# Attention and feed-forward kernel: another token order, merged tails and a different load list for the first batch

## The chip, the cores and the metric

The kernel runs on one core of a Trainium2 chip. The metric is device time in microseconds (us); three runs of the kernel before gave 718.85, 719.02 and 719.22 us, median 719.02 us. Inputs and outputs lie in the chip's memory (HBM). A core has a matrix engine (TensorE, PE), a vector engine (VectorE, DVE), an activation engine (ScalarE, ACT), a general engine (GpSimd, POOL) and a queue engine (SyncE, SP). Loads are issued from SP's and ACT's instruction streams and carried by the core's 16 DMA engines.

## The reference, cut to what matters

There are 8 batches, 8 heads, 576 tokens, head width 64, and 32 memory slots. All is float32.

```python
a   = exp(phi - max over tokens)            # phi: batch, head, token, slot
a   = a / (sum of a over tokens + 1e-9)
k_m = sum over tokens of a[token, slot] * k[token, :]      # v_m likewise with v
s   = q @ k_m.T / sqrt(64);  p = softmax(s over slots)
x   = p @ v_m                              # 4608 rows of 512 = 8 heads x 64
out = square(relu(x @ w_in)) @ w_out       # w_in 512x2048, w_out 2048x512
```

The sums over tokens do not care in which order the tokens come, so long as `phi`, `k` and `v` are taken in the same order.

## The kernel before, in words

Each batch has 576 tokens, cut in five chunks: four of 128 tokens (a token per partition) and a tail of 64 tokens (`rows(4)` is 64). `e_sb` holds `phi` as 128 partitions x 5 chunks x 256, where the 256 columns are two halves (`qd` 0 and 1) of four heads x 32 slots. `kv` holds for each batch and half of the heads 576 tokens x 4 heads x 128 (k beside v), so that a token of one half is 2 KB in a row.

For batch 0 the start is written out by hand in the string `order` (L957), whose letters step through generators:

- `e` is `exp_phi` (L166): the maximum over chunks on DVE (L170, L175), two transposes on PE (L180), a reduce (L185), a broadcast by matmul (L190), then per chunk an addition on DVE (L199) and an exponential on ACT (L201).
- `m` is `task_mem`, which runs `memories` (L322): sums of the chunks on DVE (L332, L335), 40 small matmuls (recorded as 80) for the sums over tokens (L350), first those of half 0 and then of half 1, chunk by chunk, the denominators (L357), and a division and transposes.
- `d0` to `d3` decode pieces of `w_in` (ACT L581 and L584, DVE L586 to L594, an addition at L601); `a0` is the attention of the first tokens (`first_softmax`: DVE L487 to L512, ACT L497 and L517); `u0` makes the first product for the feed-forward part.

Engines take their instructions in the order in which the program lists them. `spin` (L144) puts fillers on PE, matmuls whose result nobody reads: `spin(n, x, k=4)` is n matmuls over k blocks of 128 columns. Before the first transpose there are `spin(3, ident)` and `spin(1, ident, k=2)`, 14 blocks.

The first loads come from the list `loads` (L910): `load_phi` for batch 0 (SP takes the four whole chunks, ACT the 64-row tail), then `first_kv` for each half (three loads: chunks 0 and 1, chunks 2 and 3, tail; on ACT, SP, ACT for half 0, and on SP, SP, ACT for half 1), then the first piece of `w_in`, four loads of `q`, and further pieces of the weights. That is two loads of `phi` and six of `kv` ahead of the first weights. The data of `kv` go to tiles that are used for other things later (`u_hi3`, `u_lo3`, `u_hi4`, `wo4`, `wo5`, `wo6`). A tail tile has its unused 64 partitions set to zero by POOL (`fill`, L106). Each tail load goes to partitions 0 to 63.

After the start, steps of the feed-forward part (L677, L720, L728) run on PE by a fixed plan (`plan`, `early`, `late`), with the tasks of the following batches between them.

Of the kernel before, what the change touches and what calls it, by code (L numbers as in the profile page):

```python
# [8 lines left out]
F32 = mybir.dt.float32  # L9
# [3 lines left out]
AF = mybir.ActivationFunctionType  # L13
ALU = mybir.AluOpType
# [10 lines left out]
def attn_moe_kernel(ctx: ExitStack, tc: tile.TileContext, qT, kv, phi, w_in, w_out, outT):  # L25
# [20 lines left out]
    D = 64  # L46
# [12 lines left out]
    def rows(c):  # L59
        return min(P, S - c * P)  # L60
# [45 lines left out]
    def fill(c, t):  # L106
        if rows(c) < P:
            nc.gpsimd.memset(t[rows(c):], 0.0)
        if t.shape[-1] == CW:
            nc.gpsimd.memset(t[:rows(c), :, 2 * D:], 1.0)  # L110

    def fill_all():
        for c in range(NCH):
            fill(c, kvb[c])
            if rows(c) < P:
                nc.gpsimd.memset(e_sb[rows(c):, c], 0.0)

    ones = const.tile([P, CW - 2 * D], F32, name="ones")
    nc.gpsimd.memset(ones, 1.0)
# [24 lines left out]
    def spin(n, x, h=None, k=4):  # L144

        if h is None:
            h = ps_h.tile([P, 512], F32, name="h")
        for _ in range(n):
            nc.tensor.matmul(  # L149
                h[:, :k * P], x, ident[:, None, :].broadcast_to([P, k, P]), start=True, stop=True  # L150
            )

    def load_phi(b, nc_q=nc.sync):
        nfull = S // P
        assert b == 0 or ("read", b - 1) in ready
        nc.sync.dma_start(out=e_sb[:, :nfull], in_=phi[b, :nfull * P].rearrange("(c p) x -> p c x", p=P))
        if b > 1:
            for qd in range(NQ):
                nc_q.dma_start(
                    out=e_sb[D * qd:D * (qd + 1), nfull, :P], in_=phi[b, nfull * P:, qd * P:(qd + 1) * P]  # L160
                )
            return [e_sb[:, c] for c in range(nfull)] + [e_sb[:, nfull, :P]]
        nc_q.dma_start(out=e_sb[:rows(nfull), nfull], in_=phi[b, nfull * P:])
        return [e_sb[:rows(c), c] for c in range(NCH)]

    def exp_phi(b, e):  # L166

        w = NQ * P
        mx = one.tile([P, w], F32, name="phi_mx")
        nc.vector.tensor_tensor(out=mx, in0=e[0], in1=e[1], op=ALU.max)  # L170
        for x in e[2:]:
            n = x.shape[0]
            if fine and not starting:
                yield True
            nc.vector.tensor_tensor(out=mx[:n], in0=mx[:n], in1=x, op=ALU.max)  # L175
        yield
        ps = new_ps()
        tp, bc = bank(ps, 0), bank(ps, 1)
        for qd in range(NQ):
            nc.tensor.transpose(tp[:, qd * P:(qd + 1) * P], mx[:, qd * P:(qd + 1) * P], ident)  # L180
        if starting:
            spin(1, ident, k=2)
        yield
        nmx = work.tile([P, NQ], F32, name="nmx")
        nc.vector.tensor_reduce(  # L185
            out=nmx, in_=tp[:, :w].rearrange("p (q x) -> p q x", q=NQ), axis=AX.X, op=ALU.max, negate=True
        )
        yield
        for qd in range(NQ):
            nc.tensor.matmul(  # L190
                bc[:, qd * P:(qd + 1) * P], nmx[:, qd:qd + 1].broadcast_to([P, P]), ident,
                start=True, stop=True,
            )
        if starting:
            spin(2, nmx[:, :1].broadcast_to([P, P]))
        yield
        for x in e:
            n = x.shape[0]
            nc.vector.tensor_tensor(out=x, in0=x, in1=bc[:n, :w], op=ALU.add)  # L199
            if starting:  # L200
                nc.scalar.activation(x, x, AF.Exp)  # L201
        done_ps(ps)
        if starting:
            ready.add(("phi", b))
            return
        yield
        nfull = S // P
        nc.scalar.activation(e_sb[:, :nfull], e_sb[:, :nfull], AF.Exp)
        if nfull < NCH:
            nc.scalar.activation(e[nfull], e[nfull], AF.Exp)  # L210
        ready.add(("phi", b))

    def exp_phi_blocks(b, e):

        w = NQ * P
        nb = w // M
        mx = one.tile([P, w], F32, name="phi_mx")
        nc.vector.tensor_tensor(out=mx, in0=e[0], in1=e[1], op=ALU.max)
        for x in e[2:-1]:
            nc.vector.tensor_tensor(out=mx, in0=mx, in1=x, op=ALU.max)  # L220
        at = [(slice(D * qd, D * (qd + 1)), slice(P * qd, P * (qd + 1))) for qd in range(NQ)]
        for hs, cs in at:
            nc.vector.tensor_tensor(out=mx[hs, cs], in0=mx[hs, cs], in1=e[-1][hs], op=ALU.max)
        yield
        tr = one.tile([P, w], F32, name="at")
        nc.vector.transpose(tr, mx)
        top = work.tile([P, nb], F32, name="top")
        nc.vector.tensor_reduce(out=top, in_=tr.rearrange("p (k x) -> p k x", k=nb), axis=AX.X, op=ALU.max)
        yield
        for g in range(1, P // M):  # L230
            nc.vector.tensor_tensor(out=top[:M], in0=top[:M], in1=top[M * g:M * (g + 1)], op=ALU.max)
        for g in range(1, P // M):
            nc.vector.tensor_copy(top[M * g:M * (g + 1)], top[:M])
        yield
        nc.vector.tensor_copy(tr.rearrange("p (k x) -> p k x", k=nb), top[:, :, None].broadcast_to([P, nb, M]))
        nc.vector.transpose(mx, tr)
        yield
        for x in e[:-1]:
            nc.vector.tensor_tensor(out=x, in0=x, in1=mx, op=ALU.subtract)
        for hs, cs in at:  # L240
            nc.vector.tensor_tensor(out=e[-1][hs], in0=e[-1][hs], in1=mx[hs, cs], op=ALU.subtract)
        yield
        nfull = S // P
        nc.scalar.activation(e_sb[:, :nfull], e_sb[:, :nfull], AF.Exp)
        nc.scalar.activation(e[nfull], e[nfull], AF.Exp)
        ready.add(("phi", b))

    def load_kv(b, qd, lent=None):

        got = []  # L250
        for c in range(NCH):
            if lent:
                t = lent(c)
            elif qd and b > 1 and rows(c) < P:
                nc.sync.dma_start(out=kvb[c][D:, :, :2 * D], in_=kv[b, qd, c * P:])
                got.append(kvb[c])
                continue
            elif qd:

                name, bufs = ("tmp", 3) if c < 3 else ("low", 2)  # L260
                if b == 2 and c < 3:
                    if not c:
                        w1 = const.tile([P, 3, 4, CW], F32, name="w1")
                    t = w1[:, c]
                else:
                    t = work.tile([P, 4, CW], F32, name=name, bufs=bufs)
            else:
                t = kvb[c]
                assert c not in kv_used
                kv_used.add(c)  # L270
            if qd:
                fill(c, t)
            elif b == 2 and rows(c) < P:
                nc.gpsimd.memset(t[rows(c):, :, 2 * D:], 1.0)
            nc.sync.dma_start(out=t[:rows(c), :, :2 * D], in_=kv[b, qd, c * P:c * P + rows(c)])
            got.append(t)
        return got

# [43 lines left out]
    def memories(b, e, kvs, mem):  # L322
# [7 lines left out]
        if b == 0:  # L330
            total = one.tile([P, NQ * P], F32, name="phi_mx")
            nc.vector.tensor_tensor(out=total, in0=e[0], in1=e[1], op=ALU.add)  # L332
            for c in range(2, NCH):
                n = rows(c)
                nc.vector.tensor_tensor(out=total[:n], in0=total[:n], in1=e[c][:n], op=ALU.add)  # L335
        for qd, kvt in kvs.items():
            if b and kvt[0].shape[-1] < CW:
                for c, y in enumerate(kvt):
# [542 lines left out]
    st = state[0]  # L881
    kvs = {}

    def first_kv(qd):

        names = (("u_hi3", "u_lo3", "u_hi4"), ("wo4", "wo5", "wo6"))[qd]
        queues = ((nc.scalar, nc.sync, nc.scalar), (nc.sync, nc.sync, nc.scalar))[qd]
        got = []
        for name, nc_q in zip(names, queues):
            c = len(got)  # L890
            t = const.tile([P, 2, 4, 2 * D], F32, name=name)
            n = min(2, S // P - c)
            if n:
                x = kv[0, qd, c * P:(c + n) * P].rearrange("(c p) h x -> p c h x", p=P)
                nc_q.dma_start(out=t[:, :n], in_=x)
                got += [t[:, k] for k in range(n)]
            else:
                fill(c, t[:, 0])
                nc_q.dma_start(out=t[:rows(c), 0], in_=kv[0, qd, c * P:])
                got.append(t[:, 0])  # L900
        kvs[qd] = got

    def first_phi():
        st["phi"] = load_phi(0, nc.scalar)
# [2 lines left out]
    def next_kv():  # L907
# [1 line left out]

    loads = [  # L910
        (first_phi,),
        (first_kv, 0),
        (first_kv, 1),
        (fetch_w_in, 0, 0),
        (task_q, 0, 0),
        (task_q, 0, 1),
# [24 lines left out]

    nc.scalar.activation(ones[:1, :1], ones[:1, :1], AF.Exp, scale=0.0)
    spin(3, ident)
    spin(1, ident, k=2)
    start = {
        "e": lambda: exp_phi(0, st["phi"]),
        "m": lambda: task_mem(0, kvs),
# [283 lines left out]
```

## Time and profile before

| | |
|---|---|
| Runs | 718.85, 719.02, 719.22 us |
| Profiled execution, first to last instruction (span) | 717.0 us |
| Median of the runs less that span | 2.0 us |
| PE busy | 708.0 us (99%) |
| DVE / ACT / POOL busy | 388.6 / 332.6 / 197.6 us |
| Moved by DMA | 89.50 MB |

The profiled execution's own time is given only as its span; what lies around the span is the difference to the runs. PE's busy time takes in the fillers. Times within the trace are counted from the span's start.

### The profile page before, as it was taken

How to read it: one execution, taken by the hardware profiler on the slowest of the kernel's cores; microseconds unless marked ns; L12 is line 12 of the kernel's file. 1: busy time of each engine (PE TensorE's matmuls, PEld its weight loads, DVE VectorE, ACT ScalarE, POOL GpSimd, SP SyncE). 2: the span in 40 equal slices, each digit the busy share in tenths (PEclk: the TensorE clock that was granted, in tenths of full speed). 3: DMA queues.
4: the chain of work that ended last, by engine and by line, in shares of the span. 5: the costliest groups of instructions: out<-in, count | busy, mean ns of one | idle time of the engine just before them, and what ended most of it. 6: DMA issues, size and time to landing. Idle time of an engine off the chain costs nothing.

```text
span 717.0 us, 13710 instructions
## 1 busy us (share of the span) xinstructions
PE 708.0 (99%) x5380; PEld 617.4 (86%) x5380; DVE 388.6 (54%) x835; ACT 332.6 (46%) x644; POOL 197.6 (28%) x221
## 2 busy tenths in 40 slices
PE   9899999999999999999999999999999999999998
PEld 4477798987989998888999999888899899888997
DVE  4978787987686644445472645533573445221211
ACT  2648887875454443323442444323454244332332
POOL 1222103012320133222332334222433243223332
PEclk9999999999999999999999999999999999999999
DMA  9992435331876712083411911146221222100101
GB/s 305 390 351 93 147 138 139 123 122 37 253 243 217 199 59 69 28 230 120 147 59 43 306 69 37 59 145 171 94 89 67 90 96 96 59 1 1 59 1 37
DMA packets 63281, 89.50 MB, mean 125 GB/s; under 512 B 3888, under 2 KB 52272, under 8 KB 59632
## 3 DMA queue, kind: packets, MB, share of 16 engines
q1 hardware_dynamic: 62416, 87.52, 37.9%
q10 hardware_dynamic: 800, 1.10, 0.5%
q8 instruction: 42, 0.69, 0.4%
q14 instruction: 23, 0.19, 0.1%
HBM read 74.97 MB, written 13.63 MB: 124 GB/s over the span
## 4 chain that ended last, share of the span: by engine, by line
PE 93%; DMA 2%; DVE 2%; ACT 1%; issue 0%; POOL 0%; ACTq 0%; SPq 0%; DVEq 0%
PE acc L728 53%; PE h L677 28%; PE ps_m L408 5%; PE acc L720 3%; PE h L286 2%; DMA wo<-in_w_in 1%; DMA u_hi<-in_kv 1%; PE h L408 1%; PE h L149 1%; PE ps_m L350 0%; POOL a_lo L472 0%; DVE at L468 0%; DVE st L465 0%; DVE sm L454 0%; DVE u_lo L560 0%
## 5 line engine op out<-in xcount | busy, mean ns | idle before, releaser
L685 ACT ACTIVATE r_room<-h 128x320 f32<-128x320 f32 (+2 forms) x200 | 95.4, 477 | 262.9 <-PE h L677 256.9
L691 DVE TENSOR_TENSOR g_room<-h,r_room 128x320 f32<-128x320 f32 (+1 forms) x148 | 82.5, 558 | 238.7 <-ACT r_room L685 229.7
L728 PE MATMUL acc<-g_hi,wo 128*128 128x320 f32 (+1 forms) x1024 | 175.5, 308 | 0.0
L728 PEld LDWEIGHTS acc<-g_hi,wo 128*128 128x128 f32 x1024 | 155.6, 188 | 6.1 <-ACT r_room L685 2.5
L705 POOL TENSOR_TENSOR g_lo<-g_room,g_hi 128x320 fp32r<-128x320 f32 (+1 forms) x102 | 89.9, 882 | 223.9 <-DVE g_room L691 166.6
L728 PE MATMUL acc<-o,wo 128*128 128x512 f32 x576 | 139.9, 391 | 0.0
L728 PEld LDWEIGHTS acc<-o,wo 128*128 128x128 f32 x576 | 105.2, 188 | 21.5 <-issue 1.7
L677 PE MATMUL h<-a_hi,u_hi 128*128 128x320 f32 (+1 forms) x448 | 100.9, 306 | 0.7 <-ACT u_hi L558 0.7
L705 POOL TENSOR_TENSOR o<-g_room,o 128x512 fp32r<-128x512 f32 x48 | 62.0, 1291 | 143.7 <-PE acc L728 97.0
L728 PE MATMUL acc<-g_lo,wo 128*128 128x320 f32 (+1 forms) x512 | 100.7, 307 | 0.0
L677 PE MATMUL h<-a_hi,u_lo 128*128 128x320 f32 (+1 forms) x448 | 96.3, 296 | 0.8 <-DVE u_lo L560 0.8
L677 PE MATMUL h<-a_lo,u_hi 128*128 128x320 f32 (+1 forms) x448 | 96.1, 296 | 0.1
L677 PEld LDWEIGHTS h<-a_hi,u_hi 128*128 128x128 f32 x448 | 74.8, 189 | 23.6 <-DVE st L428 9.2
L728 PEld LDWEIGHTS acc<-g_lo,wo 128*128 128x128 f32 x512 | 81.5, 188 | 0.0
L677 PEld LDWEIGHTS h<-a_hi,u_lo 128*128 128x128 f32 x448 | 72.0, 189 | 1.9 <-DVE u_lo L560 1.9
L677 PEld LDWEIGHTS h<-a_lo,u_hi 128*128 128x128 f32 x448 | 72.2, 189 | 0.4 <-POOL a_lo L472 0.4
L701 ACT ACTIVATE g_hi<-r_room 128x320 fp32r<-128x320 f32 (+1 forms) x128 | 59.8, 467 | 7.6
L701 ACT ACTIVATE o<-r_room 128x512 fp32r<-128x512 f32 x48 | 30.4, 633 | 42.4 <-PE acc L728 42.0
L560 DVE TENSOR_TENSOR u_lo<-ps_m,u_hi 128x1024 fp32r<-128x1024 f32 (+1 forms) x29 | 34.3, 1183 | 4.6 <-ACT u_hi L558 4.1
L408 PE MATMUL ps_m<-w,mem 64*32 64x512 f32 (+1 forms) x528 | 35.6, 582 | 0.9 <-POOL w L601 0.9
L720 PE MATMUL acc<-g_hi,wo 128*128 128x256 f32 (+1 forms) x128 | 34.1, 409 | 0.0
L720 PEld LDWEIGHTS acc<-g_hi,wo 128*128 128x128 f32 x128 | 23.2, 190 | 7.0 <-issue 2.0
(175 smaller groups left out, 716.4 us busy)
## 6 DMA issues: line engine op xcount, KB each, us to landing
w<-w_f SPq DMA_DIRECT2D x24, 1024.0 KB, 4.8
wo<-in_w_in SPq DMA_DIRECT2D x16, 512.0 KB, 8.1
wo<-in_w_out SPq DMA_DIRECT2D x16, 512.0 KB, 8.0
kvb<-in_kv SPq DMA_DIRECT2D x28, 256.0 KB, 6.3
q_sb<-in_q SPq DMA_DIRECT2D x16, 320.0 KB, 6.2
out_t<-o SPq DMA_DIRECT2D x30, 160.0 KB, 1.9
e_sb<-in_phi SPq DMA_DIRECT2D x8, 512.0 KB, 6.9
w_f<-w SPq DMA_DIRECT2D x4, 1024.0 KB, 5.7
```

The source lines that it names most:

```text
L149: nc.tensor.matmul(h[:, :k * P], x, ident[:, None, :].broadcast_to([P, k, P]), start=True, stop=True)
L286: nc.tensor.matmul(acc[qd][M * j:M * (j + 1), :CW], e_sb[hs, c, col + M * j:col + M * (j + 1)], kvs[qd][c][hs, j, :], start=(c == 0), stop ...
L408: nc.tensor.matmul(out[half][M * pr:M * (pr + 1), :y.shape[-1]], mem[hs, x, pr], y, start=True, stop=True)
L560: nc.vector.tensor_tensor(out=u_lo[:, :, n0:n1], in0=ps[:, :, :n1 - n0], in1=u_hi[:, :, n0:n1].bitcast(F32), op=ALU.subtract)
L677: nc.tensor.matmul(h[:, at:at + n], u[:, qd, fs], x[:, qd], start=(i == 0), stop=(i == len(todo) - 1))
L685: nc.scalar.activation(r, h[:, :T], AF.Relu)
L691: nc.vector.tensor_tensor(out=g, in0=h[:, :T], in1=r, op=ALU.mult)
L701: nc.scalar.activation(g_hi, r, AF.Square)
L705: adder.tensor_tensor(out=g_lo, in0=g, in1=g_hi.bitcast(F32), op=ALU.subtract)
L720: nc.tensor.matmul(acc[e][:, :T], wo[f][:, e * P:(e + 1) * P], g_hi, start=first, stop=last)
L728: nc.tensor.matmul(acc[e][:, :T], wo[f][:, w, e * P:(e + 1) * P], x, start=first and x is g_hi and w == 0, stop=last and x is g_lo,)
```

## The change

For every batch the four whole chunks of a half take their tokens in another order: partition p holds tokens 4p to 4p+3 instead of p, 128+p, 256+p, 384+p. The tail of 64 tokens stays the tail.

For batch 0 besides: `phi` comes in two loads of two chunks each (SP and ACT), and its tail as one load to 128 partitions, half 0 of the columns on partitions 0 to 63, half 1 on 64 to 127, in a small tile `at`. The `kv` tails of both halves come as one load to 128 partitions (`u_hi4`). The maximum is taken two chunks at a time, and the tail is treated apart, one half of the partitions at a time. The exponentials of the tail are written into `e_sb` beside zeros that POOL sets. `spin(1, ident, k=2)` at the start is gone, which leaves 12 blocks.

```diff
 def fill_all():  ...
-                nc.gpsimd.memset(e_sb[rows(c):, c], 0.0)
+                nc.gpsimd.memset(e_sb[D:, c, :P], 0.0)
+                nc.gpsimd.memset(e_sb[:D, c, P:], 0.0)
 def load_phi(b, nc_q=nc.sync):  ...
-        nc.sync.dma_start(out=e_sb[:, :nfull], in_=phi[b, :nfull * P].rearrange("(c p) x -> p c x", p=P))
+        x = phi[b, :nfull * P].rearrange("(p c) x -> p c x", p=P)
+        if b == 0:
+            for i, q in enumerate((nc.sync, nc_q)):
+                q.dma_start(out=e_sb[:, 2 * i:2 * i + 2], in_=x[:, 2 * i:2 * i + 2])
+            tail = one.tile([P, P], F32, name="at")
+            nc.sync.dma_start(out=tail, in_=phi[b, nfull * P:].rearrange("t (q x) -> q t x", q=NQ))
+            return [e_sb[:, c] for c in range(nfull)] + [tail]
+        nc.sync.dma_start(out=e_sb[:, :nfull], in_=x)
+        if b == 1:
+            nc.gpsimd.memset(e_sb[D:, nfull, P:], 0.0)
 def exp_phi(b, e):  ...
+        if b == 0:
+            two = one.tile([P, 2, w], F32, name="st")
+            nc.vector.tensor_tensor(out=two, in0=e_sb[:, 0:2], in1=e_sb[:, 2:4], op=ALU.max)
+            nc.vector.tensor_tensor(out=mx, in0=two[:, 0], in1=two[:, 1], op=ALU.max)
+            for hs, cs in halves:
+                nc.vector.tensor_tensor(out=mx[hs, cs], in0=mx[hs, cs], in1=e[-1][hs], op=ALU.max)
 ...
+            if x.shape[-1] < w:
+                for hs, cs in halves:
+                    nc.vector.tensor_tensor(out=x[hs], in0=x[hs], in1=bc[hs, cs], op=ALU.add)
+                    nc.scalar.activation(e_sb[hs, NCH - 1, cs], x[hs], AF.Exp)
+                continue
+    def tokens_of(b, qd, c):
+        nfull = S // P
+        if c == nfull:
+            return kv[b, qd, c * P:]
+        return kv[b, qd, :nfull * P].rearrange("(p c) h x -> p c h x", p=P)[:, c]
 def load_kv(b, qd, lent=None):  ...
-            nc.sync.dma_start(out=t[:rows(c), :, :2 * D], in_=kv[b, qd, c * P:c * P + rows(c)])
+            nc.sync.dma_start(out=t[:rows(c), :, :2 * D], in_=tokens_of(b, qd, c))
-    def first_kv(qd):
 ...
+    def first_kv():
+        nfull = S // P
+        tail = const.tile([P, 4, 2 * D], F32, name="u_hi4")
+        nc.scalar.dma_start(out=tail, in_=kv[0, :, nfull * P:])
+        for qd, names in enumerate((("u_hi3", "u_lo3"), ("wo4", "wo5"))):
+            x = kv[0, qd, :nfull * P].rearrange("(p c) h x -> p c h x", p=P)
+            got = []
+            for i, (nc_q, name) in enumerate(zip((nc.scalar, nc.sync), names)):
+                t = const.tile([P, 2, 4, 2 * D], F32, name=name)
+                nc_q.dma_start(out=t, in_=x[:, 2 * i:2 * i + 2])
+                got += [t[:, k] for k in range(2)]
+            kvs[qd] = got + [tail]
-    spin(1, ident, k=2)
```

## Rows read from the trace of the kernel before

**Rows 1.** The page: busy time by engine, and DMA share in 40 slices.
```profile
PE 708.0 (99%) x5380; PEld 617.4 (86%) x5380; DVE 388.6 (54%) x835; ACT 332.6 (46%) x644; POOL 197.6 (28%) x221
...
DMA  9992435331876712083411911146221222100101
```
**Rows 2.** The chain of waits, first 60 us: start us, us, what.
```profile
1.96 8.47 DMA u_hi<-in_kv
...
11.48 8.96 DMA wo<-in_w_in
...
22.09 0.89 DVE sm L501 x2
```
**Rows 3.** Stretches: busy us of PE, PEld, DVE, ACT, POOL; clock, DMA share, GB/s.
```profile
3.00:4.00 1.00, 1.00 (x2) 0.34 (x1) 0.00 (x0) 0.74 (x1) 0.48 (x2) 1.00 1.03 366
5.00:8.00 3.00, 3.00 (x9) 1.49 (x7) 1.89 (x5) 0.00 (x0) 0.00 (x0) 1.00 1.05 373
8.00:11.00 3.00, 2.92 (x21) 1.48 (x24) 2.20 (x7) 1.51 (x5) 0.00 (x0) 1.00 1.06 293
18.00:20.00 2.00, 2.00 (x5) 0.97 (x6) 2.00 (x6) 0.82 (x2) 0.38 (x1) 1.00 1.03 414
60.00:717.00 657.00, 653.10 (x4947) 582.77 (x4945) 345.14 (x738) 303.92 (x587) 184.35 (x197) 1.00 0.34 107
```
**Rows 4.** Loads issued before 3.5 us: KB, median us to landing.
```profile
wo<-in_kv SPq DMA_DIRECT2D x2, 512.0 KB, 9.4
...
wo<-in_kv ACTq DMA_DIRECT2D x1, 128.0 KB, 8.9
e_sb<-in_phi ACTq DMA_DIRECT2D x1, 64.0 KB, 4.8
```
**Rows 5.** DMA packets from 3 to 4 us.
```profile
DMA packets 357, 0.37 MB, mean 366 GB/s; under 512 B 0, under 2 KB 357, under 8 KB 357
```
**Rows 6.** DMA packets from 5 to 8 us, and by queue (q1 SP, q10 ACT).
```profile
DMA packets 568, 1.12 MB, mean 373 GB/s; under 512 B 21, under 2 KB 21, under 8 KB 568
...
q1 hardware_dynamic: 322, 0.63, 58.6%
q10 hardware_dynamic: 246, 0.49, 46.0%
```
**Rows 7.** DMA packets from 8 to 11 us.
```profile
DMA packets 488, 0.88 MB, mean 293 GB/s; under 512 B 59, under 2 KB 59, under 8 KB 488
```
**Rows 8.** DMA packets from 18 to 20 us.
```profile
DMA packets 231, 0.83 MB, mean 414 GB/s; under 512 B 29, under 2 KB 29, under 8 KB 231
```
**Rows 9.** DMA packets from 320 to 330 us, and SP's queue.
```profile
DMA packets 2404, 1.20 MB, mean 120 GB/s; under 512 B 87, under 2 KB 2403, under 8 KB 2403
...
q1 hardware_dynamic: 2403, 1.19, 57.4%
```
**Rows 10.** DVE in order of time: start us, us, line, tiles, shapes.
```profile
5.39 0.42 DVE L170 TENSOR_TENSOR phi_mx<-e_sb 128x256 f32<-128x256 f32 x1 [5.39 <-DMA e_sb<-in_phi]
5.85 1.34 DVE L175 TENSOR_TENSOR phi_mx<-phi_mx,e_sb 128x256 f32<-128x256 f32 x3
...
20.94 0.69 DVE L594 SCALAR_TENSOR_TENSOR tmp<-wo,tmp 128x512 int32<-128x512 int32 x1
```
**Rows 11.** DVE groups of the first 60 us, by form.
```profile
L449 DVE TENSOR_TENSOR st<-st,mx 128x512 f32<-128x512 f32 x1 | 0.7, 683 | 0.0
```
**Rows 12.** PE and its weight loads in order of time.
```profile
5.79 0.34 PEld L149 LDWEIGHTS h<-ident 128*128 128x128 f32 x1 [0.52 <-issue]
6.64 0.34 PEld L149 LDWEIGHTS h<-ident 128*128 128x128 f32 x1 [0.52 <-issue]
...
8.84 1.88 PE L149 MATMUL h<-ident,nmx 128*128 128x512 f32 x4
...
11.76 1.32 PE L350 MATMUL acc<-wo,e_sb 128*32 128x128 f32 x40
```
**Rows 13.** POOL's waits before 24 us: us in total, times, longest.
```profile
POOL w L601 <- DVE tmp L594: 13.6, 1, 13.6
```

More of the change, by code (lines that the diff above doesn't have):

```diff
@@ L164, in load_phi @@
         return [e_sb[:rows(c), c] for c in range(NCH)]
+    halves = [(slice(D * qd, D * (qd + 1)), slice(P * qd, P * (qd + 1))) for qd in range(NQ)]
     def exp_phi(b, e):
@@ L169, in exp_phi @@
         mx = one.tile([P, w], F32, name="phi_mx")
[L170 to L175, printed above, removed]
+        if b == 0:
[4 more added lines that the diff above has]
+                nc.vector.tensor_tensor(out=mx[hs, cs], in0=mx[hs, cs], in1=e[-1][hs], op=ALU.max)
+        else:
+            nc.vector.tensor_tensor(out=mx, in0=e[0], in1=e[1], op=ALU.max)
+            for x in e[2:]:
+                n = x.shape[0]
+                if fine and not starting:
+                    yield True
+                nc.vector.tensor_tensor(out=mx[:n], in0=mx[:n], in1=x, op=ALU.max)
         yield
@@ L220, in exp_phi_blocks @@
             nc.vector.tensor_tensor(out=mx, in0=mx, in1=x, op=ALU.max)
-        at = [(slice(D * qd, D * (qd + 1)), slice(P * qd, P * (qd + 1))) for qd in range(NQ)]
-        for hs, cs in at:
+        for hs, cs in halves:
             nc.vector.tensor_tensor(out=mx[hs, cs], in0=mx[hs, cs], in1=e[-1][hs], op=ALU.max)
@@ L239, in exp_phi_blocks @@
             nc.vector.tensor_tensor(out=x, in0=x, in1=mx, op=ALU.subtract)
-        for hs, cs in at:
+        for hs, cs in halves:
             nc.vector.tensor_tensor(out=e[-1][hs], in0=e[-1][hs], in1=mx[hs, cs], op=ALU.subtract)
@@ L332, in memories @@
             nc.vector.tensor_tensor(out=total, in0=e[0], in1=e[1], op=ALU.add)
-            for c in range(2, NCH):
-                n = rows(c)
-                nc.vector.tensor_tensor(out=total[:n], in0=total[:n], in1=e[c][:n], op=ALU.add)
+            for x in e[2:]:
+                nc.vector.tensor_tensor(out=total, in0=total, in1=x, op=ALU.add)
         for qd, kvt in kvs.items():
@@ L882, in attn_moe_kernel @@
     kvs = {}
-    def first_kv(qd):
[L886 to L901, printed above, removed]
+    def first_kv():
[10 more added lines that the diff above has]
+            kvs[qd] = got + [tail]
     def first_phi():
@@ L911, in attn_moe_kernel @@
         (first_phi,),
-        (first_kv, 0),
-        (first_kv, 1),
+        (first_kv,),
         (fetch_w_in, 0, 0),
```

## The prediction

> **What bounds the kernel now.** I read the page first: PE is busy 708.0 of 717.0 us, and the DMA share is full in slices 2 and 3 and mostly below five tenths after the first quarter [rows 1]. Next the stretches: from 60 us to the end PE works 653.1 of 657.0 us [rows 3], so whatever the start loses or gains, nothing behind it gives back or takes away; it goes into the time one for one. Then the chain of waits over the first 60 us, which runs over transfers at first: 8.47 us of it are a `kv` load and 8.96 us a load of `w_in`, before DVE's softmax sum at 22.09 [rows 2]. So the change is judged by when the loads of batch 0 land. The last view is the count of packets per stretch, from which I take what one packet costs a DMA engine.
>
> **The price of a packet.** A stretch gives 16 engines times its length times the DMA share, divided by the packets in it that are not tiny ("under 512 B"). From 3 to 4 us: 1.03 x 16 us = 16.5 us over 357 packets of 1 KB, 46 ns each [rows 3, 5]. From 5 to 8: 1.05 x 48 = 50.4 us over 547 of 2 KB, 92 ns [rows 3, 6]. From 8 to 11: 1.06 x 48 = 50.9 us over 429, nearly all of 2 KB, 119 ns [rows 3, 7]. From 18 to 20: 1.03 x 32 = 33.0 us over 202 of 4 KB, 163 ns [rows 3, 8]. From 320 to 330, rows of 512 B: 0.574 x 160 = 91.8 us over 2316, 40 ns [rows 9].
>
> In 8 to 11 us the same 2 KB packet is 27 ns dearer, while the tails of `kv` go to partitions 0 to 63. [...]
>
> **The change, part by part.** All prices below are per DMA engine.
>
> 1. Token order, whole chunks. `phi`: before 512 packets of 1 KB, 32 per engine x 46 = 1.47 us; after 256 of 2 KB, 16 x 92 = 1.47 us. Nothing. `kv`: four loads of 256 packets of 2 KB, 64 x 92 = 5.89 us; a partition's two tokens now lie side by side, 4 KB, so 32 x 163 = 5.22 us: -0.67 us. (If they are not joined, 0.) In later batches the same loads lie under a DMA share of 0.34 [rows 3], and `kv` chunks there keep packets of 2 KB: 0, and without that cover at most 0.2 us for `phi`, for better.
>
> 2. The old tails go: `phi` 64 packets of 1 KB, 4 x 46 = 0.18 us; `kv` two of 64 packets of 2 KB, 8 x 119 = 0.95 us. And the other 301 packets of 8 to 11 us get 27 ns cheaper: 301 / 16 x 27 = 0.51 us. Together -1.64 us.
>
> 3. The new tails come: `phi` 128 packets of 512 B, `kv` 128 of 2 KB. Spread over 16 engines that is 8 x 40 + 8 x 92 = 1.06 us. But these two are the only loads in the program whose source counts 2 in its outermost place (the halves, then 64 tokens); all loads of before count 64 or 128 there. To share a load among engines it must be cut somewhere, and if it is cut along that outermost count there are only two pieces: 64 x 40 + 64 x 92 = 8.45 us on two engines, nothing on the other 14. No row shows a load with an outer count of 2, so both ends stay open: +1.06 and +8.45 us. By distance the nearest rows, the old 64-row tails, which land in 4.8 and 8.9 us [rows 4], speak for the first end. I take the second: those rows have an outer count that 16 divides, so they can't tell the two apart, and here the cut at 2 is the only one that the source's outermost count offers.
>
> [...]
>
> Every other load has a share on those two engines and lands when the last engine has done its share. So all that queues behind the tails (`kv`, then `w_in`, `q`) is later by 8.45 - 0.67 - 1.64 = 6.1 us.
>
> 4. What the path makes of 6.1 us. The last `kv` loads, issued on SP, land 9.4 us after issue [rows 4], about when the 40 matmuls of half 1 start at 11.76 [rows 12]: no slack for them. From there everything in the hand-written order is later by as much. One place absorbs something: DVE ends a decode step at 21.63 and waits for the exponentials until 22.09 [rows 2, 10], 0.46 us. Net +5.6 us.
>
> 5. The maximum. `phi_mx` needs the tail of `phi`. Before it runs from 5.39 to 7.19 [rows 10]. After: one operation on 128x512, 0.68 us [rows 11], one on 128x256, 0.42, and two on 64x128, by the slope of these two rows 0.29 each: 1.68 us if all has landed, 0.58 us behind the tail. If the two engines do the `phi` tail first it lands 64 x 40 = 2.6 us after the whole chunks (about 5.3), the maximum ends at 8.5, +1.3 us; if they alternate with the `kv` tail on the other queue, 8.45 us after, ends at 14.3, +7.1 us. The queues shared evenly from 5 to 8 us (58.6% and 46.0%) [rows 6], so it will be nearer the second, but this wait runs beside that of point 4 and is not added to it.
>
> 6. Two more small DVE additions and one more exponential on ACT: 5 x 0.42 becomes 4 x 0.42 and 2 x 0.29, +0.2 us, hidden by the fill of 1.88 us on PE ahead of the first L350 [rows 12]; without that cover 0.2 us. POOL: two memsets fewer and one more, while POOL stands 13.6 us [rows 13]: 0. The small memset for batch 1 waits for batch 0's matmuls and is queued ahead of decode additions on POOL: 0 to 0.3 us. Eight loads are issued ahead of `w_in` before and after, four on SP and four on ACT: 0, between -0.3 and +0.3 us.
>
> 7. Two filler blocks fewer. While filling, PE's weight loads come every 0.85 us, 0.34 us each [rows 12], so these two blocks are about 0.85 us. They end at about 6.7 instead of 7.5; PE then waits for the maximum, 0 on the path. If PE falls back to that slow pace after standing, the fill of 1.88 us, four records [rows 12], takes 4 x 0.85 = 3.4 us, 1.5 us more; bounds 0 to +1.5, I take 0, as the data of point 4 is late anyway.
>
> Sum: +5.6 us in the trace. The median stands 2.0 us above the span, and I take that as unchanged: 719.0 + 5.6 = 724.6 us.
>
> **Rivals.**
> A. The tails are shared by all 16 engines. Then point 3 is +1.06, the queue is 1.06 - 0.67 - 1.64 = 1.25 us shorter, but the tail of `phi`, behind the whole chunks and beside the `kv` tail, lands about 1.06 us after 5.3, at 6.4, and the maximum ends at 6.9 instead of 7.2. The path takes the smaller gain, 0.2 to 1.2 us, say 0.6: 718.4 us. For it: the old tails did spread. Against: nothing but the outer count of 2. This is the case that is not slower; what decides is into how many pieces the load is cut: the gains of points 1 and 2 and the slack, 0.67 + 1.64 + 0.46 = 2.8 us, pay for 2.8 / (0.040 + 0.092) = 21 packets of each tail on an engine, which is 128 packets on six; on fewer engines it turns to slower.
> B. The maximum is what ends last, and PE falls to the slow pace: +7.1 + 1.5 - 0.5 = +8.1 us, 727.1 us. For it: the even sharing of the queues [rows 6] and the slow pace before 7 us [rows 12]. Against: nothing shows PE slowing after a stand.
> C. Two engines, but the start has slack I don't see, so that little arrives: 719 to 720.5 us. Against: L350 follows its data at once.
>
> **How the numbers follow.** Two tails on two engines as in the sum 0.50 (723 to 726.3); B 0.20 (726.3 to 729); A 0.24, a sixth of it beyond 0.2%; C 0.06. About 0.2%, 1.4 us, is what a measurement of this kernel tells from no change: faster 0.04, same 0.26, slower 0.70. Cases of both signs hold the chance, so the range of 8 in 10 runs from 718.2, within A, to 727.4, within B. Without A and C it is 723.0 to 727.4.
>
> **What would show it.** In the profile of the changed kernel: the loads of the tails take 9 us or more to land; the DMA share falls well below 1 between 6 and 14 us, as 14 engines run out of work while two go on; the L350 matmuls of half 1 start 5 to 7 us later than 11.76; PE stands idle ahead of L180 or L350. If instead `at` lands by 6.5 us, the share stays at 1 and those matmuls start by 11.8, A is right and the cut by the outer count is wrong. If the tails land late and the time stays, C.

## The result, and the profile after

The changed kernel takes 729.44 us (median of 4 runs, 727.06 to 730.36) against 719.08 us (718.85 to 719.22) for the kernel before in the same comparison: ratio 1.014, 95% interval 1.0123 to 1.0157. It is slower by 10.4 us; 724.6 us was forecast, with a range up to 727.4. The profiled execution took 729.9 us, of which 728.1 us are the span, 11.1 us more than before; the runs stand 1.8 us above their own spans, and so do those of the kernel before; the 2.0 us of the prediction is a median less the span of another execution. One execution of x3_kv_16 and the profiled one of w_order_alone, both below, were disturbed (1161 and 2450 us); the ratios leave them out.

The page of the changed kernel first: busy time by engine, then the granted clock and the DMA share in 40 slices.

```profile
PE 709.1 (97%) x5378; PEld 617.8 (85%) x5378; DVE 389.5 (53%) x836; ACT 333.0 (46%) x645; POOL 197.1 (27%) x221
...
PEclk7999999999999999999999999999999999999999
DMA  7993418152494921137222832127421222100101
```

PE is busy for as long as before, within 1.1 us [rows 1]; the time has gone into idle PE, and the clock's first slice says where. The stretches of the changed kernel (busy us of PE, PEld, DVE, ACT, POOL; clock, DMA share, GB/s):

```profile
4.00:5.00 1.00, 1.00 (x3) 0.40 (x2) 0.60 (x1) 0.68 (x2) 0.00 (x0) 1.00 0.59 107
6.00:10.00 4.00, 0.85 (x1) 0.00 (x0) 0.00 (x0) 0.00 (x0) 0.00 (x0) 1.00 1.04 317
10.00:12.00 2.00, 0.00 (x0) 0.00 (x0) 0.00 (x0) 0.00 (x0) 0.00 (x0) 0.61 1.04 304
12.00:14.00 2.00, 0.00 (x0) 0.00 (x0) 0.00 (x0) 0.00 (x0) 0.00 (x0) 0.50 0.89 296
14.00:16.00 2.00, 0.00 (x0) 0.00 (x0) 0.00 (x0) 0.00 (x0) 0.00 (x0) 0.50 0.72 224
16.00:18.00 2.00, 1.23 (x4) 0.79 (x4) 0.97 (x3) 0.00 (x0) 0.00 (x0) 0.50 0.31 76
20.00:22.00 2.00, 2.00 (x16) 0.78 (x18) 1.83 (x7) 1.95 (x7) 0.00 (x0) 0.83 0.91 275
70.00:728.00 658.00, 654.15 (x4952) 583.68 (x4950) 346.06 (x739) 304.94 (x589) 184.84 (x197) 1.00 0.34 107
```

From 70 us to the end PE idles 3.9 us in all, as it did from 60 us on before [rows 3]: nothing behind the start gives anything back. From PE's last filler, which ends at 6.85, to 16 us no engine computes. The DMA share, which stayed at 1 before [rows 3], sinks to 0.31 from 16 to 18 us. SP's stream stands meanwhile, 7.7 us for `u_hi` and 2.6 us for `at`, before it issues more loads of `q`. In order of time DVE shows the wait (start us, us, line, tiles, shapes; in brackets the idle time before, and what ended it):

```profile
4.40 0.69 DVE L184 TENSOR_TENSOR st<-e_sb 128x512 f32<-128x512 f32 x1 [4.40 <-DMA e_sb<-in_phi]
5.13 0.42 DVE L185 TENSOR_TENSOR phi_mx<-st 128x256 f32<-128x256 f32 x1
16.43 0.61 DVE L187 TENSOR_TENSOR phi_mx<-phi_mx,at 64x128 f32<-64x128 f32 x2 [10.88 <-DMA at<-in_phi]
```

And PE, in order of time:

```profile
1.36 5.49 PE L150 MATMUL h<-ident 128*128 128x512 f32 x6 [1.36 <-POOL ones L120]
16.77 0.80 PE L199 MATMUL acc<-ident,phi_mx 128*128 128x128 f32 x2 [9.93 <-DVE phi_mx L187]
...
19.10 2.67 PE L150 MATMUL h<-ident,nmx 128*128 128x512 f32 x4
21.71 0.64 PE L378 MATMUL acc<-u_hi,e_sb 128*32 128x128 f32 x16
...
22.82 1.06 PE L378 MATMUL acc<-wo,e_sb 128*32 128x128 f32 x32
...
24.03 0.61 PE L385 MATMUL acc<-ones,phi_mx 128*128 128x2 f32 x4
```

The whole chunks of `phi` are there at 4.40 us, a microsecond before the 5.39 of [rows 10]; the tail holds the maximum up for 10.88 us. The maximum ends at 17.04 instead of 7.19: +9.85 us. The first of the small matmuls (L378, before L350) start 4.67 us after that; before they started at 10.65, 3.46 us after (the first of the two rows below). Together that is 9.85 + 1.21 = +11.06 us, the span's whole difference. I put the 1.21 us down to the clock, which x4 below tests: PE stood from 6.85 to 16.77 us, the granted clock fell to 0.50 in that time, and the fill of four records took 2.67 us where it took 1.88 [rows 12]; the other 0.4 us lie ahead of the fill. PE of the kernel before:

```profile
10.65 0.64 PE L350 MATMUL acc<-u_hi,e_sb 128*32 128x128 f32 x16
...
13.01 0.61 PE L357 MATMUL acc<-ones,phi_mx 128*128 128x2 f32 x4
```

The loads issued before 3.5 us (KB, us to landing):

```profile
u_lo<-in_kv SPq DMA_DIRECT2D x1, 512.0 KB, 15.5
u_hi<-in_kv ACTq DMA_DIRECT2D x1, 512.0 KB, 12.3
wo<-in_kv SPq DMA_DIRECT2D x1, 512.0 KB, 16.1
wo<-in_kv ACTq DMA_DIRECT2D x1, 512.0 KB, 13.4
e_sb<-in_phi ACTq DMA_DIRECT2D x1, 256.0 KB, 3.6
```

The two whole loads of `kv` on SP's queue, behind the `phi` tail, take 15.5 and 16.1 us, those on ACT's queue, behind the `kv` tail, 12.3 and 13.4; before, the loads of `wo` took 9.4 us [rows 4]. Of the tails themselves this view shows no landing; that of `phi` is read from the wait of L187 above.

### The profile page after: what moved, and what is told of

The parts are those of the page before. It is cut to its first block, busy times and chain, and to the rows that moved or that the text cites. A ratio compares the mean times of both kernels' runs of the same rounds, so it can differ in the third digit from the quotient of the medians.

```text
span 728.1 us, 13710 instructions
## 1 busy us (share of the span) xinstructions
PE 709.1 (97%) x5378; PEld 617.8 (85%) x5378; DVE 389.5 (53%) x836; ACT 333.0 (46%) x645; POOL 197.1 (27%) x221
## 2 busy tenths in 40 slices
DMA packets 59861, 89.50 MB, mean 123 GB/s; under 512 B 3860, under 2 KB 48212, under 8 KB 56212
## 4 chain that ended last, share of the span: by engine, by line
PE 91%; DMA 5%; SPq 1%; DVE 1%; ACT 0%; POOL 0%; issue 0%; DVEq 0%
PE acc L756 52%; PE h L705 28%; PE ps_m L436 4%; PE acc L748 3%; DMA wo<-in_kv 2%; PE h L315 2%; DMA wo<-in_w_out 1%; DMA wo<-in_w_in 1%; SPq L304 1%; PE h L436 1%; DMA u_hi<-in_kv 1%; PE ps_m L378 0%; POOL a_lo L500 0%; DVE at L496 0%; DVE st L493 0%
## 5 line engine op out<-in xcount | busy, mean ns | idle before, releaser
(181 smaller groups left out, 719.0 us busy)
```

## The experiments

Unless a sentence says otherwise, each kernel is the changed one with one edit. I take the start of the denominators (L385, before L357) for the end of the start-up; the span follows it to within 0.6 us. The times up to the span are of one profiled execution each:

| kernel | tails on engines (phi, kv) | maximum ends | first L378 | L385 starts | span | median us |
|---|---|---|---|---|---|---|
| before | 16, 16 | 7.19 | 10.65 | 13.01 | 717.0 | 719.0 |
| after | 2, 2 | 17.04 | 21.71 | 24.03 | 728.1 | 729.44 |
| x1_tails_16 | 16, 16 | 6.60 | 9.87 | 12.88 | 716.9 | 719.26 |
| x2_phi_16 | 16, 2 | 6.48 | 18.04 | 22.41 | 726.6 | 727.19 |
| x3_kv_16 | 2, 16 | 10.30 | 15.91 | 18.27 | 722.5 | 723.49 |
| x4_fill_14 | 2, 2 | 16.51 | 19.77 | 22.22 | 726.3 | 728.34 |
| y_pieces_8 | 8, 8 | 8.30 | 11.57 | 14.20 | 718.8 | 722.32 |
| y_pieces_4 | 4, 4 | 12.56 | 17.84 | 20.16 | 724.5 | 726.15 |

The second column is my estimate by the outermost count, as in point 3, not a reading of its own. The trace's records of single packets bear it out: the 128 packets of the `kv` tail are under way mostly two at a time in the changed kernel (from 3.95 to 12.54 us), mostly four in y_pieces_4 (3.92 to 7.69), and up to 16 or more in x1 (3.77 to 5.14).

**Both tails re-laid.** The same bytes come from two extra input arrays that hold the tails as 128 rows, so that the source's outermost count is 128.

```diff
-            nc.sync.dma_start(out=tail, in_=phi[b, nfull * P:].rearrange("t (q x) -> q t x", q=NQ))
+            nc.sync.dma_start(out=tail, in_=phi_tail)
-        nc.scalar.dma_start(out=tail, in_=kv[0, :, nfull * P:])
+        nc.scalar.dma_start(out=tail, in_=kv_tail)
```

> Both merged tails are read from arrays of their own with 128 rows, so that the outermost count of the source is 128 instead of 2; loads, queues, instructions and bytes are those of the changed kernel. Theory (a load is cut along its outermost count, two pieces go to two engines, and the path waits for the tail of phi): the tails cost an engine 8 x 40 + 8 x 92 ns = 1.1 us instead of 8.5, the tail of phi lands by 6.5 us, PE doesn't stand, 718.4 us (717.5 to 719.5). Rival (the new token order or the load list makes the loads slow): stays at 727 to 730.

719.26 us (718.71 to 720.44), ratio to before 1.0005, interval 0.9996 to 1.0014. The whole loss is gone with nothing changed but the shape of two sources. In this kernel the tails do have landing rows:

```profile
u_hi<-in_kv_tail ACTq DMA_DIRECT2D x1, 256.0 KB, 4.3
at<-in_phi_tail SPq DMA_DIRECT2D x1, 64.0 KB, 3.9
```

And in PE's order of time:

```profile
11.65 1.08 PE L378 MATMUL acc<-wo,e_sb 128*32 128x128 f32 x32 [0.48 <-DMA wo<-in_kv]
...
12.88 0.61 PE L385 MATMUL acc<-ones,phi_mx 128*128 128x2 f32 x4
```

The maximum ends 0.59 us earlier than before, but half 1 of `kv` then is what PE waits for, and 0.13 us are left.

**One tail each.** In x2 only the `phi` tail is re-laid, in x3 only the `kv` tail: one of the two edits above.

> Only the tail of phi is read from an array with 128 rows; the kv tail still has an outermost count of 2. Theory: the maximum ends at about 7.2 us as before; the kv tail's 64 x 92 = 5.9 us on two engines make everything behind it 5.9 + 0.3 - 1.1 - 0.7 - 0.5 = 3.9 us later, less 0.5 of slack: 722.5 us (721 to 724.5). Rival (the path waits for the tail of phi alone): as with both tails on 16 engines, 718 to 719.5.

> Only the kv tail is read from an array with 128 rows; the tail of phi still has an outermost count of 2. Theory: its 64 packets of 512 B on two engines alternate with what ACT's queue has for them (8 of 2 KB, 16 of 4 KB): 2.6 + 0.7 + 2.6 us behind 4.2, landing near 10.1, the maximum ends at 10.7 instead of 17.0: 722.8 us (721 to 725). Rival (the kv tail is what costs): 718 to 720.

x2: 727.19 us, ratio 1.0111 (1.0096 to 1.0126), far above what I expected. x3: 723.49 us, ratio 1.0058 (1.0043 to 1.0073), as expected. By the ratios their excess is 0.0111 x 718.92 = 8.0 and 0.0058 x 718.92 = 4.2 us, together 12.2, more than the 10.4 of both at once, so the two partly lie beside each other. PE of x2:

```profile
18.04 1.08 PE L378 MATMUL acc<-u_hi,e_sb 128*32 128x128 f32 x16 [8.24 <-DMA u_hi<-in_kv]
...
22.41 0.61 PE L385 MATMUL acc<-ones,phi_mx 128*128 128x2 f32 x4
```

Its loads to landing:

```profile
u_lo<-in_kv SPq DMA_DIRECT2D x1, 512.0 KB, 7.8
wo<-in_kv SPq DMA_DIRECT2D x1, 512.0 KB, 9.9
u_hi<-in_kv ACTq DMA_DIRECT2D x1, 512.0 KB, 15.5
wo<-in_kv ACTq DMA_DIRECT2D x1, 512.0 KB, 16.5
```

And its stretches:

```profile
12.00:14.00 2.00, 0.00 (x0) 0.00 (x0) 0.13 (x1) 0.00 (x0) 0.00 (x0) 0.51 0.67 235
14.00:16.00 2.00, 0.00 (x0) 0.00 (x0) 0.00 (x0) 1.21 (x2) 0.00 (x0) 0.50 0.15 58
```

Here the maximum is early (6.48 us), and the wait is for whole chunks of half 0 that stand behind the `kv` tail in ACT's queue. From 14 to 16 us the DMA share is 0.15; two engines of 16 are 0.125. The same-sized loads on SP's queue landed 7.8 and 9.9 us after issue, so they went past the tail; the two behind it in ACT's queue took 15.5 and 16.5 us. My 722.5 us had counted the tail's own 64 x 92 ns and not what the two engines do for SP's queue meanwhile. That packets of both queues alternate, the packet records of the changed kernel show: from 7 to 12 us they have 69 packets of the `phi` tail and 68 of the `kv` tail, for the most part one by one in turn.

In x3 DVE waits for the `phi` tail alone, and PE's fill is slow:

```profile
9.70 0.60 DVE L187 TENSOR_TENSOR phi_mx<-phi_mx,at 64x128 f32<-64x128 f32 x2 [4.05 <-DMA at<-in_phi]
```

```profile
12.36 3.62 PE L150 MATMUL h<-ident,nmx 128*128 128x512 f32 x4
```

**Pieces.** The same arrays, read as 8 x 16 rows or as 4 x 32, out of larger ones so that the rows can't be joined; the outermost count is then 8 or 4.

```diff
-            nc.sync.dma_start(out=tail, in_=phi_tail)
+            nc.sync.dma_start(out=tail, in_=phi_tail[:, :P // 8])
-        nc.scalar.dma_start(out=tail, in_=kv_tail)
+        nc.scalar.dma_start(out=tail, in_=kv_tail[:, :P // 8])
```

> Both tails from arrays of their own, laid out with a gap so that the source's outermost count is 8 (8 pieces of 16 rows). Theory (pieces = outermost count, one engine each, and an engine alternates packet by packet between the two queues): 16 packets of each tail on eight engines, 2.1 us instead of 1.1, half 1's first kv data about 1 us later than with 16: 720.2 us (719.2 to 721). Rival (only the count 2 is special, or any source in pieces is slow): like 16 engines (719.3) or like the changed kernel (729).

> As before with an outermost count of 4 (4 pieces of 32 rows). Theory: 32 packets of each tail on four engines, 4.2 us instead of 1.1, the tail of phi lands about 9 and the kv data behind the tails 3.2 us later: 722.5 us (721 to 724.5). Rival: 719.3 or 729.

8: 722.32 us, ratio 1.0041 (1.0027 to 1.0055). 4: 726.15 us, ratio 1.0095 (1.0081 to 1.0109). Both medians are dearer than I expected. The trace of y_pieces_8 is of an execution of 720.6 us, as expected; the other three took 722.2 to 722.6, and what they lost more no trace shows. But the order is that of the outer count: 128, 8, 4, 2 give 719.3, 722.3, 726.2, 729.4 us, with the same bytes to the same partitions. DVE in y_pieces_8, then in y_pieces_4:

```profile
7.70 0.60 DVE L187 TENSOR_TENSOR phi_mx<-phi_mx,at 64x128 f32<-64x128 f32 x2 [2.06 <-DMA at<-in_phi_tail]
```

```profile
11.95 0.61 DVE L187 TENSOR_TENSOR phi_mx<-phi_mx,at 64x128 f32<-64x128 f32 x2 [6.35 <-DMA at<-in_phi_tail]
```

DVE's wait goes 10.88, 6.35, 2.06 us and, in x1, none. The four runs agree with the cut along the outermost count that point 3 took, and x2's DMA share of 0.15 fits its two engines.

**PE kept busy.** Eleven more fillers ahead of the maximum, so that PE doesn't stand.

```diff
-    spin(3, ident)
+    spin(14, ident)
```

> The changed kernel with 11 more filler matmuls of 4 blocks ahead of the first transpose, so that PE works until about 16.7 us. Theory (1.2 us of the loss are PE at half its clock after standing): the granted clock stays at 1.0, from the end of the maximum to the first sum over tokens it takes 3.5 us instead of 4.7, and 728.2 us (727 to 729.3). Rival (the clock has no share): 729.4 and 4.7 us.

728.34 us, ratio 1.013 (1.0116 to 1.0143). PE of this kernel, then one of its stretches:

```profile
17.96 1.88 PE L150 MATMUL h<-ident,nmx 128*128 128x512 f32 x4
19.77 0.64 PE L378 MATMUL acc<-u_hi,e_sb 128*32 128x128 f32 x16
```

```profile
12.00:14.00 2.00, 2.00 (x6) 0.88 (x5) 0.00 (x0) 0.00 (x0) 0.00 (x0) 1.00 0.98 329
```

The clock stays at 1.00, the fill is back at 1.88 us, and from the maximum's end (16.51) to the first L378 it is 3.26 us instead of 4.67. So the clock's 1.2 to 1.4 us are shown. The medians of this kernel and of the changed one, 1.1 us apart, were taken beside different runs of before, and their runs overlap (728.84 against 727.06 at the edges); the trace settles it, not the medians.

**Why x1 is not faster than before.** The first two chunks of half 1 on SP's queue, the last two on ACT's (x1 with `(nc.sync, nc.scalar)` for half 1), since x1 waits for the load that ACT issues last:

```diff
-            for i, (nc_q, name) in enumerate(zip((nc.scalar, nc.sync), names)):
+            for i, (nc_q, name) in enumerate(zip((nc.scalar, nc.sync) if qd == 0 else (nc.sync, nc.scalar), names)):
```

> Both tails from arrays with 128 rows (16 engines), and for half 1 the first two chunks on SP's queue and the last two on ACT's. With 16 engines PE stood 0.48 us ahead of half 1's first chunk, which came on ACT's queue at 11.6 us, while SP's queue was through at 11.2. Theory (with the tails spread what is left is the order of the kv data): the stand goes, at most 0.45 us less than 719.26: 718.8 us (718.3 to 719.3), which may not be told from before. Rival (nothing left to gain there): 719.3.

718.60 us (718.04 to 719.28), ratio 0.9996 (0.9987 to 1.0005): not told from before. The wait is gone:

```profile
11.16 1.06 PE L378 MATMUL acc<-wo,e_sb 128*32 128x128 f32 x32
...
12.49 0.61 PE L385 MATMUL acc<-ones,phi_mx 128*128 128x2 f32 x4
```

L385 starts 0.52 us before its place in the kernel before, and the span is 0.3 us shorter (716.7): about what the change would be worth with its tails on all engines and this order of queues, and too little for these runs to tell.

**The tails without extra arrays.** Each merged tail as two loads to 64 partitions each, into the same tiles; all queues as in the changed kernel.

```diff
-            nc.sync.dma_start(out=tail, in_=phi[b, nfull * P:].rearrange("t (q x) -> q t x", q=NQ))
+            for qd in range(NQ):
+                nc.sync.dma_start(out=tail[D * qd:D * (qd + 1)], in_=phi[b, nfull * P:, qd * P:(qd + 1) * P])
-        nc.scalar.dma_start(out=tail, in_=kv[0, :, nfull * P:])
+        for qd in range(NQ):
+            nc.scalar.dma_start(out=tail[D * qd:D * (qd + 1)], in_=kv[0, qd, nfull * P:])
```

> The changed kernel with the original arrays, but each merged tail as two loads, one per half of the heads (64 rows to 64 partitions each, outermost count 64). Two loads more ahead of the weights. Theory: all engines share them, 719.5 us (718.8 to 720.5). Rival (merging or the load list, not the count of 2, made it slow): 727 to 730.

720.41 us, ratio 1.0023 (1.0013 to 1.0034): 9 us of the 10.4 come back by this alone. The profiled execution took 721.8 us, 1.4 more than the median, so its rows show more than the median lost. What is left in it, first in PE's order of time, then in the loads issued from 4 to 6 us:

```profile
12.94 1.08 PE L379 MATMUL acc<-wo,e_sb 128*32 128x128 f32 x32 [1.48 <-DMA wo<-in_kv]
...
14.64 3.65 PE L150 MATMUL h<-ident 128*128 128x512 f32 x4
```

```profile
wo<-in_kv SPq DMA_DIRECT2D x1, 512.0 KB, 7.7
wo<-in_kv ACTq DMA_DIRECT2D x1, 512.0 KB, 7.9
```

With ten loads ahead of the weights in place of eight, the last two of `kv` are issued only as the loads of `phi` land, at 4.71 and 4.96 us (in the changed kernel the last of the eight is issued at 2.71), and PE waits for them; the fill after that wait takes 3.65 us at a granted clock of 0.66 and 0.50, where x1's takes 1.96. Whether the executions near the median have the slow fill no trace shows.

**The token order alone, and the fillers alone.** The kernel before with `"(p c) x -> p c x"` and its likes for `phi` and `kv`, all else as before; and x1 with `spin(1, ident, k=2)` put back.

> The kernel before with the token order of the four whole chunks alone changed (all batches); loads, tails and fillers as before. Theory (the whole loss lies in the two tails that two DMA engines carry): no loss; the joined tokens of kv may spare 0.67 us of the queue, of which the path takes 0 to 0.6: 718.7 us (718.2 to 719.3). Rival (the order itself costs something, in later batches too, where it was priced at nothing): 720 us or more.

> The kernel with both tails re-laid to 128 rows (16 engines), and the two filler blocks back, so 14 as before. Theory (fillers matter only where PE stands long): the same as with 12 blocks, 719.3 us (718.6 to 719.8). Rival (the two fillers fewer keep the gain of the earlier data from the path): 718.2 us or less.

719.49 us, ratio 1.0008 (0.9999 to 1.0017), and 719.07 us, ratio 1.0002 (0.9993 to 1.0011). Neither can be told from before. The token order costs nothing that can be measured, and the 0 to 0.6 us of gain that I had left open for it don't show; its median lies 0.2 us above the range I gave. The two fillers are worth nothing where PE doesn't stand.

## Why the prediction was wrong

The direction and the mechanism were right; the size was not, and the forecast took the wrong one of two waits as the last.

- **Point 3, two engines: right.** x1 and the series of pieces show it: with 128 rows in the sources nothing is left of the loss (719.26 us, ratio 1.0005).
- **Point 4, the path over `kv`: right as a size, but it did not set the end.** In the chain of waits of the changed kernel the last `kv` load on SP's queue takes 16.05 us from issue. Before, the last one took 9.9 (the 9.4 of [rows 4] is the median of 8.8 and 9.9), so 6.15 us more; I had 6.1. (First the changed kernel: start us, us, what; then the load before: KB, us to landing.)

```profile
2.65 16.05 DMA wo<-in_kv
```

```profile
wo<-in_kv SPq DMA_DIRECT2D x1, 512.0 KB, 9.9
```

  It landed at 18.70, and PE, held up by the maximum, came to that half only at 22.82, 4.1 us later. The size fits where both queues have such a tail at their head. In x2, where only ACT's has, the same reckoning gave 3.9 us and the excess was 8.0.
- **Point 5, the failed step.** "This wait runs beside that of point 4 and is not added to it" holds, but the longer of two waits side by side is the one that counts, and I gave the forecast the shorter one. My upper end for it, +7.1 us, already exceeded the 6.1 of point 4, and I had called it the nearer one. And its size was short: +9.85 us. I counted 64 x 40 + 64 x 92 = 8.45 us on the two engines, as if they carried the tails alone. ACT's queue also holds two whole `kv` loads of 4 KB packets, 8 per engine each if 16 engines share them evenly, and by this estimate the two engines carry these between the packets of SP's tail: 16 x 163 ns = 2.6 us. The packet records have 30 packets of ACT's whole loads from 12.5 to 15.5 us, for the most part one by one in turn with those of the `phi` tail. From the 4.40 us at which the whole chunks had landed, 8.45 us would give 12.9, with these 15.5; DVE went on at 16.43.

  The records of single packets have most of the missing microsecond. From the first packet of the `kv` tail (about 3.95 us) to the end of the last one of the `phi` tail (15.71) it is 11.76 us, where the sum has 8.45 + 2.6 = 11.05: the `kv` tail's packets took 113 ns each on average, and I had counted 92. The records also show why the whole `kv` loads got in between. The `phi` tail's first packet starts only at 6.20 us, when 46 of the `kv` tail's 128 have started, so the `phi` tail lasts 3.2 us longer than the `kv` tail, and in that time the loads behind the `kv` tail take the turns. In x1 all 128 packets of the `phi` tail have started by 4.7 us; they are of 512 B, so they count as under 2 KB but not as under 512 B. Packets of the changed kernel from 0 to 6.2 us, then of x1 from 0 to 4.7:

```profile
DMA packets 437, 1.03 MB, mean 167 GB/s; under 512 B 34, under 2 KB 34, under 8 KB 437
```

```profile
DMA packets 580, 0.92 MB, mean 197 GB/s; under 512 B 58, under 2 KB 186, under 8 KB 580
```

  Why the `phi` tail starts so late stays open.
- **Point 7, the clock: taken as 0, it was +1.2 us.** The reason given, that the data of point 4 is late anyway, fell with point 4: behind the maximum the fill is on the path. x4 shows the size. The bound of +1.5 held; the two fillers themselves are nothing, as x1 with 14 blocks shows.
- **Rival B was what happened,** at 0.20, with its price too low: 7.1 + 1.5 - 0.5 = 8.1 us forecast, 9.85 + 1.21 = 11.06 in the trace. The 0.46 us of slack that it took off were not there to take: L385 is late by 11.02 us and the span by 11.1.
- **Points 1, 2 and 6: small.** Two 64x128 operations on DVE take 0.61 us, I had 2 x 0.29; one on 128x512 takes 0.69, I had 0.68. The order of the tokens shows as nothing, the gain of points 1 and 2 in the queue (1.25 us after the tails' own cost on 16 engines) as at most the 0.5 us by which L385 comes earlier in x1_swap_queues. The 27 ns that point 2 expects back no run shows: from 8 to 10 us x1 moves 414 GB/s at a DMA share of 1.02, where before it was 293 from 8 to 11 [rows 3], but its whole `kv` loads are of other packets (4 KB); and in the changed kernel, whose tails go to 128 partitions too, 202 packets of 4 KB took 212 ns each from 8 to 11 us, where I had counted 163.
- **Rival A,** 718.4 us if 16 engines share the tails: x1 gives 719.26. That rival had the maximum as the smaller gain (0.3 us); in x1 the maximum gains 0.59 us, and it is the data of half 1 that gains less. Even then the change would have been no gain that these runs can tell.
- **The signs.** The late tail and the standing PE came. The matmuls of half 1 started at 22.82, 11.1 us later than 11.76 instead of 5 to 7. The DMA share stayed at 1.04 until 12 us and fell below 0.8 only from 14 on: the other 14 engines still had `w_in` and `q` to move, issued from 4.40 us on.

## What to carry to other kernels

Before two loads are merged to fill 128 partitions, look at the outermost count of the source: here one that is 2, on two small loads (64 and 256 KB), left the packets of the second mostly two at a time under way and cost 10 us (4 us with the first alone, 8 with the second alone), while two loads of 64 partitions for each gave back 9 of them. Price a load that few engines carry with everything that these engines also do for the other queue, and with all that stands behind it in its own (in x2 15.5 and 16.5 us to landing behind the tail, 7.8 and 9.9 on the other queue). And where two waits run side by side, work each of them through to the end and forecast with the longer, the time of an engine that stands meanwhile included.

## What the runs showed that I had not expected

- The granted clock fell to 0.50 while PE stood from 6.85 to 16.77 us, and was back at 1.00 only after some microseconds of work: 0.50 still from 16 to 20 us, 0.83 from 20 to 22, 1.00 from 22 to 24. In w_split_loads a wait of 1.48 us on PE was followed by a fill at 0.66 and 0.50, in x1 one of 0.48 us was not.
- The `kv` tail, cut in few pieces, took longer to issue here, and the DMA share sank behind it. From 4 to 5 us the DMA share of the changed kernel is 0.59 with 107 GB/s, in x4_fill_14 0.38, in y_pieces_8 0.73, but in x1 1.07 with 398 GB/s; and ACT's instruction that issues the tail (L916, the row below) takes 1.12 us in place of 0.45. All five kernels with that tail in 2, 4 or 8 pieces show it (1.11 to 1.18 us), and none of the others that issue it as one load (0.45); whether the two belong together, and what they cost, no run separated. The missing microsecond of point 5 it is not, as the `kv` tail's own packets start at about 3.95 us here and at 3.77 in x1. The `phi` tail's start may hang on it: 3.40 us in x1, 4.32 in x3, 6.20 here.

```profile
L916 ACTq DMA_DIRECT2D u_hi<-in_kv x1: 1120/1120/1120, 1.2 to 1.2; - x1
```

- Two tokens of `kv` that lie side by side do come as one packet of 4 KB: in the packet records ACT's two whole `kv` loads are 256 packets of 4 KB, and before its queue has none of that size in the first 25 us. In all, the changed kernel moves the same 89.50 MB in 59861 packets, the kernel before in 63281; most of that difference is `phi`.
